# Splitting the float32 operands of the q, k and v projections into two float16 parts each, in a two-layer attention and router kernel

## The chip, the cores and the metric

The kernel runs on one core of a Trainium2 chip. The metric is the device time of one execution in microseconds (us); less is better. A core has a matrix engine (PE; its weight loads are shown apart as PEld), a vector engine (DVE), a scalar engine (ACT), a general-purpose engine (POOL) and an engine that issues DMA transfers (SP). Each engine works through its own instructions in order and waits where a semaphore is not yet up. A matrix product leaves its result in PSUM banks. POOL cannot read PSUM.

## The reference, cut to what matters

```python
x = x + A(layernorm(x));  x = x + B(layernorm(x))      # and the same pair once more
def A(x):            # 2048 tokens of 512, 32 heads of 16, one shared key and value head
    q = (x @ wq) per head;  k = x @ wk;  v = x @ wv
    p = softmax(q k^T * 16 ** -0.5);  return (p v) @ wo
def B(x):            # a router picks the 2 tokens with the greatest x . w_r
    return x + (a gated feed-forward net on these two tokens alone)
```

All inputs are float32.

## The kernel before, in words

The 2048 tokens are 16 tiles of 128. `xT` holds the normalised input transposed (four blocks of 128 features by 2048 tokens), `wq_sb` and `wkv_sb` the weights; all three are float32. Queries are needed in 16 groups `G` (4 chunks of 512 tokens by 4 groups of heads).

**Head.** Tiles are loaded, `in_stats` takes mean and variance on DVE and the reciprocal root (`rstd_of`, six small instructions) on POOL, `in_norm` normalises on DVE (`ln_x`), transposes on PE and copies to `xT` on ACT (`ln_t`). The tiles go in five groups: g0 and g1 of two tiles, g2 to g4 of four. After g1 the first query projection runs (`q_proj`, 256 tokens). After each chunk of four tiles `kv_piece` makes keys and values: PE, two ACT copies, one POOL subtraction (`kp`), then the keys go through DRAM (`k_store`, `k_spread`) into `k_st`. The piece of the last chunk is made in `early`, the first thing in layer 0.

**Stream of a layer.** 512 steps; in each, four score units (PE product, ACT exponential) and four units of row maxima (PE product `max_mm`, L458; DVE `reduce_max`, L469). A lead of eight steps has maxima alone. After every three score units (a run) PE does the products with the values (`pv_mm`, L557) and then, through `between`, at most one step of a pending piece: a step of the next query group (`q_piece`, four steps a piece, 60 pieces a layer) or of the output projection (`o_piece`). `by_columns` (L192) lays one step over the four column groups of PE. The order of all engines is that of the program text; nothing is rescheduled.

**Keys of chunk 1 less chunk 0.** `kd_x` subtracts inputs on POOL, `kd_tile` projects the difference; four tiles a layer.

**In layer 0 also** the tiles of layer 1 are normalised beside the stream (`next_x`, `ln_t`, `kv_piece`), the last four at its end. POOL does most of this. After the stream the router picks its two tokens (a gather from `xl_d`), the net runs, the two rows are normalised again, and layer 1 begins.

Float32 products are written as one instruction in the program and appear in the trace as two weight loads and two matmuls.

Of the kernel before, what the change touches and what calls it, by code (L numbers as in the profile page):

```python
# [17 lines left out]
P = 128  # L18
# [8 lines left out]
NG = 4  # L27
# [30 lines left out]
def interleaved_layers(ctx, tc, x_in, wq, wkv, wo, w_r, w_gate, w_up, w_down, out):  # L58
# [49 lines left out]
    xT = const.tile([P, NDC, S], F32, name="xT")  # L108
    wq_sb = const.tile([P, NDC, D], F32, name="wq_sb")
    wkv_sb = const.tile([P, NDC, P], F32, name="wkv_sb")  # L110
# [32 lines left out]
    def load_wq(w):  # L143
        return wq_sb[:, :, w], wq.rearrange("(c p) n -> p c n", p=P)[:, :, w]
# [30 lines left out]
    nc.gpsimd.memset(v_exts[0], 1.0)  # L175

# [91 lines left out]
    def kv_piece(c, pool=True):  # L268


        def step(k):
            def f(out, start, stop, shared):
                for j in range(TPC):
                    i = c * TPC + j
                    nc.tensor.matmul(out[32 * j:32 * (j + 1)], wkv_sb[:, k, 2 * DH:HR], xT[:, k, i * P:(i + 1) * P],
                                     start=start, stop=stop, skip_group_check=shared)
# [39 lines left out]
    def q_proj(G, w=slice(0, CW)):  # L316
# [18 lines left out]
    def q_piece(G, w):  # L335
# [3 lines left out]
        def step(k):  # L339
            def f(out, *flags):  # L340
                by_columns(out, wq_sb[:, k, g * P:(g + 1) * P], xT[:, k, c * CW + w.start:c * CW + w.stop], *flags)
# [13 lines left out]
    def k_direct(li, i):  # L355
# [3 lines left out]
        for k in range(NDC):  # L359
            nc.tensor.matmul(pk, wkv_sb[:, k, :], xT[:, k, w], start=k == 0, stop=k == NDC - 1)  # L360
# [10 lines left out]
    kds = {}  # L371

    def kd_x(li, j):

        w = slice(j * P, (j + 1) * P)
        kds[li, j] = xd = work.tile([P, NDC, P], F32, name="xh", bufs=3)
        nc.gpsimd.tensor_tensor(xd, xT[:, :, CW + w.start:CW + w.stop], xT[:, :, w], op=OP.subtract)

    def kd_tile(li, j):

        xd = kds.pop((li, j))
        w = slice(S + j * P, S + (j + 1) * P)
        pk = aux([P, P], F32)
        for k in range(NDC):
            nc.tensor.matmul(pk, wkv_sb[:, k, :], xd[:, k, :], start=k == 0, stop=k == NDC - 1)
        kf = work.tile([P, P], F32, name="kvf", bufs=2)
        nc.scalar.copy(kf, pk)
# [5 lines left out]
    def v_direct(li, i):  # L393
        w = slice(i * P, (i + 1) * P)
        pv = aux([P, DH], F32)
        for k in range(NDC):
            nc.tensor.matmul(pv, xT[:, k, w], wkv_sb[:, k, KQ:HR], start=k == 0, stop=k == NDC - 1)
# [15 lines left out]
    def layer(li, src_d, dst_d, early=None):  # L413
# [586 lines left out]
        for j in range(TPC):  # L1000
            at(T_KD + 2 * j, kd_x, li, j)
# [71 lines left out]
        if nxt:  # L1073
            ln_t(i - 2)
# [160 lines left out]
        ln_t(i - 1)  # L1235
        ln_t(i)
# [5 lines left out]
        for k in range(NDC):  # L1242
# [7 lines left out]
        xn = work.tile([P, NDC, 2], F32, name="xn", bufs=1)  # L1250
        nc.vector.tensor_copy(xn, pxn)
# [4 lines left out]
        for tok in toks:  # L1256
            of = nc.snap(tok // P)
            xb.append((of, work.tile([P, NDC, P], F32, name="xh", bufs=3)))
            nc.gpsimd.tensor_copy(xb[-1][1], xT[:, :, bass.ds(of * P, P)])
# [5 lines left out]
        for k in range(NDC):  # L1265
            nc.tensor.matmul(pk, wkv_sb[:, k, :], xn[:, k, :], start=k == 0, stop=k == NDC - 1)
# [14 lines left out]
        def v_again(of, x):  # L1281
            pv = aux([P, 1, DH], F32)
            for k in range(NDC):
                nc.tensor.matmul(pv[:, 0, :], x[:, k, :], wkv_sb[:, k, KQ:HR], start=k == 0, stop=k == NDC - 1)
# [16 lines left out]
    def in_norm(of):  # L1301
        for i in of:
            ln_x(i, xin[i], mvs[of], i - of[0], rss[of], nc.vector)
            ln_t(i)
# [17 lines left out]
    in_norm(g2)  # L1322
# [7 lines left out]
    in_norm(g3)  # L1330
# [3 lines left out]
    in_norm(g4)  # L1334
# [7 lines left out]

    number_tokens()
# [31 lines left out]
```

## Time and profile before

| | |
|---|---|
| median of 3 runs | 2670.74 us (2668.63 to 2672.21) |
| profiled execution | 2668.52 us |
| its span, first to last instruction | 2666.7 us |
| busy PE, DVE, ACT, POOL | 2611.8, 2496.2, 2336.5, 789.6 us |
| mean granted clock of PE | 0.987 of full speed |

Busy shares are means over a head, two streams and two tails. Matmuls overlap and their ends are modelled, so a busy PE is not one at its limit. A row of the trace gives the start, the length, the engine and line, the tiles written and read, how many were merged, and in brackets the idle time before and what ended it.

### The profile page before, as it was taken

How to read it: one execution, taken by the hardware profiler on the slowest of the kernel's cores; microseconds unless marked ns; L12 is line 12 of the kernel's file. 1: busy time of each engine (PE TensorE's matmuls, PEld its weight loads, DVE VectorE, ACT ScalarE, POOL GpSimd, SP SyncE). 2: the span in 40 equal slices, each digit the busy share in tenths (PEclk: the TensorE clock that was granted, in tenths of full speed). 3: DMA queues.
4: the chain of work that ended last, by engine and by line, in shares of the span. 5: the costliest groups of instructions: out<-in, count | busy, mean ns of one | idle time of the engine just before them, and what ended most of it. 6: DMA issues, size and time to landing. Idle time of an engine off the chain costs nothing.

```text
span 2666.7 us, 94903 instructions
## 1 busy us (share of the span) xinstructions
PE 2611.8 (98%) x39844; PEld 1264.3 (47%) x39844; DVE 2496.2 (94%) x4499; ACT 2336.5 (88%) x4874; POOL 789.6 (30%) x2144
## 2 busy tenths in 40 slices
PE   7999999999999999999999999999999999999999
PEld 3544444444444444444555444444444444444445
DVE  8999999999999999999679999999999999999995
ACT  2899999999999999999728999999999999999995
POOL 2211101234162433535522111012331424233363
PEclk7999999999999999999979999999999999999999
DMA  3001110000100001111400000000001000000114
GB/s 100 6 23 34 33 58 11 13 12 31 31 28 17 19 19 30 33 31 34 142 15 6 15 15 13 30 11 15 10 31 31 31 12 27 21 20 31 31 50 132
DMA packets 71344, 83.15 MB, mean 31 GB/s; under 512 B 27932, under 2 KB 44252, under 8 KB 70916
## 3 DMA queue, kind: packets, MB, share of 16 engines
q1 hardware_dynamic: 68050, 75.80, 9.4%
q8 instruction: 313, 5.13, 0.8%
q10 hardware_dynamic: 2354, 1.07, 0.1%
q14 instruction: 115, 0.94, 0.1%
q0 software_dynamic: 512, 0.20, 0.0%
HBM read 42.80 MB, written 17.18 MB: 22 GB/s over the span
## 4 chain that ended last, share of the span: by engine, by line
PE 68%; ACT 17%; POOL 5%; issue 5%; DMA 3%; DVE 2%; SPq 1%; ACTq 0%; DVEq 0%; POOLq 0%
PE pO L557 29%; PE pS L528 20%; ACT pr L530 13%; PE pM L458 9%; PE pO L192 5%; DMA q_st<-mr 1%; ACT wd L462 1%; SPq L507 1%; POOL xh L711 1%; ACT so L563 1%; ACT qf L687 1%; PE pS L192 1%; DVE mx L469 1%; DMA x<-xl_d,of 1%; POOL xh L773 0%
## 5 line engine op out<-in xcount | busy, mean ns | idle before, releaser
L469 DVE TENSOR_REDUCE mx<-pM 128x1 f32<-128x512 f32 x3784 | 2315.1, 680 | 86.4 <-PE pM L458 76.3
L530 ACT ACTIVATE pr<-pS 128x512 f32<-128x512 f32 x4044 | 2134.9, 609 | 183.7 <-PE pM L458 141.2
L458 PE MATMUL pM<-k_st,q_st 48*128 48x512 f16 x4096 | 1234.7, 386 | 7.3 <-DVE mx L469 3.3
L528 PE MATMUL pS<-q_st,k_st 50*128 50x512 f16 (+1 forms) x4248 | 1186.9, 371 | 21.4 <-DMA q_st<-mr 5.1
L557 PE MATMUL pO<-pr,v_ext 128*32 128x128 f32 (+1 forms) x22528 | 1174.2, 327 | 5.7 <-ACT so L563 2.2
L557 PEld LDWEIGHTS pO<-pr,v_ext 128*32 128x32 f32 x22528 | 561.8, 109 | 611.1 <-issue 387.7
L528 PEld LDWEIGHTS <-k_st 50*128 50x128 f16 x4352 | 298.6, 95 | 495.7 <-issue 371.6
L458 PEld LDWEIGHTS <-q_st 48*128 48x128 f16 x4096 | 295.8, 94 | 166.8 <-issue 133.6
L493 POOL TENSOR_SCALAR ma<-ma 128x8 f32<-128x8 f32 (+1 forms) x136 | 32.4, 238 | 834.4 <-DVE ma L488 627.5
L192 PE MATMUL pO<-xT,wq_sb 128*32 128x128 f32 x3840 | 192.6, 273 | 0.0
L688 POOL TENSOR_TENSOR x<-x,qf 128x128 f32<-128x128 f32 x128 | 58.3, 457 | 426.5 <-ACT qf L687 426.2
L192 PE MATMUL pO<-wo_sb,so 128*32 128x128 f32 x3328 | 162.0, 273 | 0.0
L350 POOL CAST qh<-qf 128x128 f16<-128x128 f32 x120 | 35.0, 292 | 423.6 <-ACT qf L349 423.6
L192 PEld LDWEIGHTS pO<-xT,wq_sb 128*32 128x32 f32 x3840 | 119.2, 110 | 34.4
L192 PEld LDWEIGHTS pO<-wo_sb,so 128*32 128x32 f32 x3328 | 102.4, 110 | 28.5
L711 POOL TENSOR_TENSOR xh<-xh 128x128 f32<-128x128 f32 (+7 forms) x384 | 98.6, 257 | 30.1
L466 DVE CUSTOM_DVE_ANT_0 wd<-pM,wd 128x512 f32<-128x512 f32 x156 | 106.1, 680 | 0.0
L462 ACT ACTIVATE wd<-pM 128x512 f32<-128x512 f32 x156 | 94.7, 607 | 0.0
L773 POOL TENSOR_TENSOR xh<-xh 128x256 f32<-128x256 f32 (+8 forms) x216 | 66.8, 309 | 15.0
L563 ACT COPY so<-pO 128x256 f32<-128x256 f32 (+1 forms) x136 | 54.3, 400 | 1.6 <-PE pO L557 1.5
L351 POOL TENSOR_TENSOR ql<-qf,qh 128x128 f16<-128x128 f32 x120 | 51.6, 430 | 9.7
L757 POOL TENSOR_SCALAR xh<-x,mv,rs 128x512 f32<-128x512 f32 x24 | 50.1, 2088 | 0.0
(268 smaller groups left out, 1061.9 us busy)
## 6 DMA issues: line engine op xcount, KB each, us to landing
q_st<-mr SPq DMA_DIRECT2D x512, 1.0 KB
zt<-zr_d SPq DMA_DIRECT2D x120, 64.0 KB
q_st<-qh SPq DMA_DIRECT2D x236, 32.0 KB
xl_d<-xh SPq DMA_DIRECT2D x28, 256.0 KB
pr<-in_w_up SPq DMA_DIRECT2D x12, 448.0 KB
x<-in_x SPq DMA_DIRECT2D x20, 256.0 KB
x_d<-x SPq DMA_DIRECT2D x16, 256.0 KB
x<-x_d SPq DMA_DIRECT2D x16, 256.0 KB
```

The lines of the kernel that those rows point to most:

```text
L192: nc.tensor.matmul(out[r], lhsT[:, r], rhs, start=start, stop=stop, skip_group_check=shared)
L458: nc.tensor.matmul(pm, q_st[u][r, j, q:q + P], k_st[r, kc * CW:(kc + 1) * CW], start=True, stop=True)
L462: nc.scalar.activation(rect, pm, AF.Relu)
L466: nc.vector.tensor_tensor_reduce(out=b_over_a, in0=pm, in1=b_over_a, scale=1.0, scalar=LOWEST, op0=OP.add, op1=OP.max, accum_out=mx[u][:, ...
L469: nc.vector.reduce_max(mx[u][:, c, i:i + 1], pm, axis=AX.X)
L528: nc.tensor.matmul(ps[:, k * 2 * w:(k + 1) * 2 * w], k_st[rows, kt * P:(kt + 1) * P], q_st[u][rows, :, b * w:(b + 1) * w], start=True, sto ...
L530: nc.scalar.activation(pr[hs][:, h, :], ps, AF.Exp, scale=DH ** -0.5)
L557: nc.tensor.matmul(po[u][32 * j:32 * (j + 1), b * w + q.start:b * w + q.stop], v_ext[:, kt, 1 - u % 2:33 - u % 2], p[:, j % 2, k, j // 2, ...
L563: nc.scalar.copy(so[u][:, b * w:(b + 1) * w], po[u][:, b * w:(b + 1) * w])
L688: nc.gpsimd.tensor_tensor(x1[i][:, w], x1[i][:, w], y, op=OP.add)
L711: g.tensor_tensor(t[:, :n], t[:, :n], t[:, n:2 * n], op=OP.add)
L773: nc.gpsimd.tensor_tensor(rp_t[i][:, :n], rp_t[i][:, :n], rp_t[i][:, n:2 * n], op=OP.add)
```

## The change

Every normalised input and weight of these projections is kept as a high and a low float16 part (low is the rest, rounded). A product becomes three float16 products: high by high, and the two mixed ones.

- Weights are loaded to staging tiles and split on POOL (`split_w`: a cast and a subtraction), `wkv` behind the first memsets, group 0 of `wq` before g2's `rstd_of`, groups 1 to 3 behind the head. The loads of groups 1 to 3 are three transfers in place of one.
- `ln_t` takes three forms. With `low=nc.vector` (g0, g1; the last two tiles of layer 0) ACT casts the high part and DVE subtracts from PSUM. With `low=nc.gpsimd` (g2 to g4; tile 13) ACT casts and copies, POOL subtracts. With none (in the stream) ACT copies once, POOL casts and subtracts.
- Query, key and value products run 12 float16 products where 4 float32 ones stood; `kd_x` is gone, `kd_tile` projects both chunks and POOL subtracts the two results.

```diff
-    xT = const.tile([P, NDC, S], F32, name="xT")
+    xT = const.tile([P, 2, NDC, S], HF, name="xT")
...
+    def split_w(name, dst):
+
+        w = staged.pop(name)
+        nc.gpsimd.tensor_copy(dst[:, 0], w)
+        nc.gpsimd.tensor_tensor(dst[:, 1], w, dst[:, 0], op=OP.subtract)
...
+    def by_parts(out, lhsT, rhs, start, stop, shared=False):
+
+        pairs = ((0, 0), (0, 1), (1, 0))
+        for n, (a, b) in enumerate(pairs):
+            by_columns(out, lhsT[:, a], rhs[:, b], start and n == 0, stop and n == len(pairs) - 1, shared)
+
+    def dot(out, lhsT, rhs, low_last):
+
+        pairs = ((0, 0), (1, 0), (0, 1)) if low_last else ((0, 0), (0, 1), (1, 0))
+        for n, (a, b) in enumerate(pairs):
+            for k in range(NDC):
+                nc.tensor.matmul(out, lhsT[:, a, k], rhs[:, b, k], start=n == k == 0, stop=n == 2 and k == NDC - 1)
...
-    def ln_t(i):
+    def ln_t(i, low=None):
+
         pT = aux([P, NDC, P], F32)
+        xh = xhs.pop(i)
         for c in range(NDC):
-            nc.tensor.transpose(pT[:, c, :], xhs[i][:, c * P:(c + 1) * P], ident)
-        nc.scalar.copy(xT[:, :, i * P:(i + 1) * P], pT)
-        del xhs[i]
+            nc.tensor.transpose(pT[:, c, :], xh[:, c * P:(c + 1) * P], ident)
+        hi, lo = (xT[:, a, :, i * P:(i + 1) * P] for a in range(2))
+        xh = xh.rearrange("p (c n) -> p c n", c=NDC)
+        if low:
+            nc.scalar.copy(hi, pT)
+        if low is nc.vector:
+            xh = pT
+        else:
+            nc.scalar.copy(xh, pT)
+        if not low:
+            nc.gpsimd.tensor_copy(hi, xh)
+        (low or nc.gpsimd).tensor_tensor(lo, xh, hi, op=OP.subtract)
...
-        for k in range(NDC):
-            by_columns(pq, wq_sb[:, k, g * P:(g + 1) * P], xT[:, k, c * CW + w.start:c * CW + w.stop],
-                       k == 0, k == NDC - 1)
+            by_parts(pq, wq_sb[:, :, k, g * P:(g + 1) * P], xT[:, :, k, c * CW + w.start:c * CW + w.stop],
+                     k == 0, k == NDC - 1)
...
-        nc.gpsimd.tensor_tensor(xd, xT[:, :, CW + w.start:CW + w.stop], xT[:, :, w], op=OP.subtract)
...
+        pk = aux([P, 2, P], F32)
+        dot(pk, wkv_sb, xT[:, :, :, :2 * CW].rearrange("p a c (t n) -> p a c t n", t=2)[:, :, :, :, j * P:(j + 1) * P],
+             True)
+        kf = work.tile([P, NDC, P], F32, name="xh", bufs=3)
+        nc.scalar.copy(kf[:, 0:2], pk)
+        nc.gpsimd.tensor_tensor(kf[:, 2], kf[:, 1], kf[:, 0], op=OP.subtract)
...
-        for k, tok in enumerate(toks):
-            nc.scalar.copy(xT[:, :, bass.ds(tok, 1)], pxn[:, :, k:k + 1])
+        xn = work.tile([P, 2, NDC, 2], HF, name="xn", bufs=1)
+        nc.vector.tensor_copy(xn[:, 0], pxn)
+        nc.vector.tensor_tensor(xn[:, 1], pxn, xn[:, 0], op=OP.subtract)
+        for k, tok in enumerate(toks):
+            nc.scalar.copy(xT[:, :, :, bass.ds(tok, 1)], xn[:, :, :, k:k + 1])
...
-    in_norm(g2)
+    in_norm(g2, nc.gpsimd)
...
+    for g in range(1, NG):
+        split_wq(g)
     number_tokens()
     layer(0, x_in, x2_d, early)
```

The order of POOL in the head, before, from the third chunk's key subtraction to the last chunk's (`kp`; `code` and `token` are small tables of token numbers):

```order
L286 TENSOR_TENSOR kp<-kvf,kp 128x128
L102 MEMSET code 128x3
L103 MEMSET token 128x3
L106 IOTA code 14x1 x2
L106 IOTA code 128x1 x2
L106 IOTA token 128x1 x2
L286 TENSOR_TENSOR kp<-kvf,kp 128x128
```

And of the change, at the same place (`so_158` to `so_162` are staged weights):

```order
L327 TENSOR_TENSOR kp<-kvf,kp 128x128
L303 TENSOR_TENSOR xT<-xh,xT 128x4x128 x4
L153 CAST wq_sb<-so_158 128x4x128
L154 TENSOR_TENSOR wq_sb<-so_158,wq_sb 128x4x128
L153 CAST wq_sb<-so_160 128x4x128
L154 TENSOR_TENSOR wq_sb<-so_160,wq_sb 128x4x128
L153 CAST wq_sb<-so_162 128x4x128
L154 TENSOR_TENSOR wq_sb<-so_162,wq_sb 128x4x128
L102 MEMSET code 128x3
L103 MEMSET token 128x3
L106 IOTA code 14x1 x2
L327 TENSOR_TENSOR kp<-kvf,kp 128x128
```

(Two rows of the number tables, which are as before, fall between the last two.) Ten POOL instructions of 512 elements a partition now stand between the two key subtractions.

The order of DVE in the head, before, where the first four tiles are normalised:

```order
L257 TENSOR_SCALAR xh<-pr,mv,rs 128x512 x2
L246 BN_STATS st<-pr 128x6
L247 BN_AGGR mv<-st 128x2
L246 BN_STATS st<-pr 128x6
L247 BN_AGGR mv<-st 128x2
L257 TENSOR_SCALAR xh<-pr,mv,rs 128x512 x2
```

And of the change (`xT<-pS,xT` is the subtraction from PSUM):

```order
L285 TENSOR_SCALAR xh<-pr,mv,rs 128x512
L303 TENSOR_TENSOR xT<-pS,xT 128x4x128
L285 TENSOR_SCALAR xh<-pr,mv,rs 128x512
L303 TENSOR_TENSOR xT<-pS,xT 128x4x128
L274 BN_STATS st<-pr 128x6
L275 BN_AGGR mv<-st 128x2
L274 BN_STATS st<-pr 128x6
L275 BN_AGGR mv<-st 128x2
L285 TENSOR_SCALAR xh<-pr,mv,rs 128x512
L303 TENSOR_TENSOR xT<-pM,xT 128x4x128
L285 TENSOR_SCALAR xh<-pr,mv,rs 128x512
L303 TENSOR_TENSOR xT<-pM,xT 128x4x128
```

A normalisation of the next tile now stands behind the subtraction of the tile before it.

## Rows read from the trace of the kernel before

**Rows 1.** The page's busy times and shares of the span, over the whole execution.

```profile
PE 2611.8 (98%) x39844; PEld 1264.3 (47%) x39844; DVE 2496.2 (94%) x4499; ACT 2336.5 (88%) x4874; POOL 789.6 (30%) x2144
```

**Rows 2.** Busy time of each engine in stretches of 50 us (the head, the start of the stream, two stretches within it, the tail of layer 0); behind the engines the granted clock, the DMA share and GB/s.

```profile
0.00:50.00 50.00, 32.53 (x290) 17.51 (x291) 37.41 (x80) 13.15 (x32) 18.96 (x70) 0.89 0.40 131
50.00:100.00 50.00, 49.35 (x748) 27.16 (x747) 49.03 (x86) 34.04 (x71) 5.87 (x19) 0.83 0.02 4
...
200.00:250.00 50.00, 49.52 (x750) 22.88 (x754) 49.37 (x89) 46.79 (x98) 4.26 (x17) 1.00 0.11 31
...
450.00:500.00 50.00, 49.72 (x784) 23.67 (x783) 48.36 (x87) 46.45 (x98) 6.04 (x21) 1.00 0.07 19
...
1350.00:1400.00 50.00, 47.22 (x371) 25.48 (x370) 39.09 (x78) 10.84 (x28) 7.65 (x22) 0.62 0.04 9
```

**Rows 3.** Who waited for whom, whole execution: us in total, times, longest.

```profile
DVE mx L469 <- PE pM L458: 76.3, 166, 1.1
...
PE pM L458 <- DVE mx L469: 3.3, 11, 0.6
```

**Rows 4.** POOL in the head, in order of time: the second memset, the key subtractions of chunk 0 and of the last chunk, and the first and the last of the six instructions of g3's reciprocal root.

```profile
5.36 0.53 POOL L175 MEMSET v_ext<- 128x528 f32 x1
...
19.08 0.64 POOL L286 TENSOR_TENSOR kp<-kvf,kp 128x128 f16<-128x128 f32 x1 [2.77 <-ACT kp L285]
19.80 0.29 POOL L221 TENSOR_SCALAR ve<-mv 128x4 f32<-128x4 f32 x1
...
22.27 0.20 POOL L226 TENSOR_TENSOR rs<-y,t 128x4 f32<-128x4 f32 x1
...
33.32 0.43 POOL L286 TENSOR_TENSOR kp<-kvf,kp 128x128 f16<-128x128 f32 x1 [3.36 <-DMA k_st<-k_d]
```

**Rows 5.** The other engines in the head, in order of time: normalisation, transposes and copy of the first tiles, the first query projection, the third chunk's keys, the start of the maxima.

```profile
10.82 0.97 DVE L257 TENSOR_SCALAR xh<-pr,mv,rs 128x512 f32<-128x512 f32 x2
11.39 1.97 PE L262 MATMUL pS<-ident,xh 128*128 128x128 f32 x8 [8.19 <-DVE xh L257]
...
12.54 0.59 ACT L263 COPY xT<-pS 128x512 f32<-128x512 f32 x1 [9.45 <-PE pS L262]
...
15.69 1.93 PE L192 MATMUL pM<-xT,wq_sb 128*32 128x256 f32 x32
...
26.22 1.88 PE L275 MATMUL pM<-xT,wkv_sb 128*32 128x128 f32 x32
...
33.81 9.65 DVE L469 TENSOR_REDUCE mx<-pM 128x1 f32<-128x512 f32 x16 [0.45 <-PE pM L458]
```

**Rows 6.** From the arrival of the last keys to the first exponential, in order of time (PEld rows are weight loads of four matmuls, one round of the query projection).

```profile
39.63 2.08 PE L458 MATMUL pM<-k_st,q_st 48*128 48x512 f16 x4 [0.31 <-DMA k_st<-k_d]
...
41.64 3.64 PE L192 MATMUL pS<-xT,wq_sb 128*32 128x256 f32 x32
42.07 0.20 PEld L192 LDWEIGHTS pS<-xT,wq_sb 128*32 128x32 f32 x4 [0.23 <-issue]
...
56.84 3.07 ACT L530 ACTIVATE pr<-pS 128x512 f32<-128x512 f32 x5 [6.69 <-PE pS L528]
```

**Rows 7.** Groups of instructions with shapes kept apart, whole execution: count, then busy us and mean ns of one, then idle before.

```profile
L192 PE MATMUL pO<-xT,wq_sb 128*32 128x128 f32 x3840 | 192.6, 273 | 0.0
L192 PEld LDWEIGHTS pO<-xT,wq_sb 128*32 128x32 f32 x3840 | 119.2, 110 | 34.4
...
L351 POOL TENSOR_TENSOR ql<-qf,qh 128x128 f16<-128x128 f32 x120 | 51.6, 430 | 9.7
L350 POOL CAST qh<-qf 128x128 f16<-128x128 f32 x120 | 35.0, 292 | 423.6 <-ACT qf L349 423.6
...
L377 POOL TENSOR_TENSOR xh<-xT 128x512 f32<-128x512 f32 x8 | 10.2, 1280 | 0.5
...
L674 DVE TENSOR_TENSOR x<-pS,x 128x512 f32<-128x512 f32 x6 | 4.1, 691 | 11.9 <-PE pS L192 11.9
```

**Rows 8.** One run of the stream on PE, in order of time: values, a query step, the next scores.

```profile
203.31 0.86 PE L557 MATMUL pO<-pr,v_ext 128*32 128x128 f32 x16
203.98 0.40 PE L192 MATMUL pO<-xT,wq_sb 128*32 128x128 f32 x8
204.32 0.39 PE L528 MATMUL pS<-q_st,k_st 50*128 50x512 f16 x1
```

**Rows 9.** One of DVE's gaps in the stream.

```profile
456.97 0.69 DVE L469 TENSOR_REDUCE mx<-pM 128x1 f32<-128x512 f32 x1 [0.61 <-PE pM L458]
```

**Rows 10.** POOL near the end of layer 0's stream, in order of time: it works without a pause from the first of these rows to the second.

```profile
1248.63 2.09 POOL L757 TENSOR_SCALAR xh<-x,mv,rs 128x512 f32<-128x512 f32 x1
...
1278.55 0.23 POOL L493 TENSOR_SCALAR ma<-ma 128x4 f32<-128x4 f32 x1 [1.08 <-DVE ma L488]
```

**Rows 11.** POOL between the layers: its last addition before the gather, and the gather.

```profile
1316.93 1.27 POOL L780 TENSOR_TENSOR x<-x,xh 128x512 f32<-128x512 f32 x1
1319.17 1.47 POOL L807 DMA_INDIRECT x<-xl_d,of  x1 [0.97 <-DVE of L805]
```

**Rows 12.** The chain that ended last, between the layers (start, us, what): the gather's transfer, a key product and a value product.

```profile
1319.17 8.89 DMA x<-xl_d,of
...
1330.45 1.71 PE pS L360 x8
...
1371.23 1.82 PE pS L397 x8
```

More of the change, by code (lines that the diff above doesn't have):

```diff
@@ L272, in f @@
             def f(out, start, stop, shared):
[L273 to L276, printed above, removed]
+                for n, (a, b) in enumerate(((0, 0), (1, 0), (0, 1))):
+                    for j in range(TPC):
+                        i = c * TPC + j
+                        nc.tensor.matmul(out[32 * j:32 * (j + 1)], wkv_sb[:, a, k, 2 * DH:HR],
+                                         xT[:, b, k, i * P:(i + 1) * P], start=start and n == 0, stop=stop and n == 2,
+                                         skip_group_check=shared)
             return f
@@ L340, in f @@
             def f(out, *flags):
-                by_columns(out, wq_sb[:, k, g * P:(g + 1) * P], xT[:, k, c * CW + w.start:c * CW + w.stop], *flags)
+                by_parts(out, wq_sb[:, :, k, g * P:(g + 1) * P], xT[:, :, k, c * CW + w.start:c * CW + w.stop], *flags)
             return f
@@ L358, in k_direct @@
         pk = aux([P, P], F32)
-        for k in range(NDC):
-            nc.tensor.matmul(pk, wkv_sb[:, k, :], xT[:, k, w], start=k == 0, stop=k == NDC - 1)
+        dot(pk, wkv_sb, xT[:, :, :, w], True)
         def parts():
@@ L369, in k_direct @@
         return parts
[L371 to L376, printed above, removed]
-        nc.gpsimd.tensor_tensor(xd, xT[:, :, CW + w.start:CW + w.stop], xT[:, :, w], op=OP.subtract)
     def kd_tile(li, j):
-        xd = kds.pop((li, j))
         w = slice(S + j * P, S + (j + 1) * P)
[L383 to L387, printed above, removed]
+        pk = aux([P, 2, P], F32)
[4 more added lines that the diff above has]
+        nc.gpsimd.tensor_tensor(kf[:, 2], kf[:, 1], kf[:, 0], op=OP.subtract)
+        kf = kf[:, 2]
         for h in range(2):
@@ L395, in v_direct @@
         pv = aux([P, DH], F32)
-        for k in range(NDC):
-            nc.tensor.matmul(pv, xT[:, k, w], wkv_sb[:, k, KQ:HR], start=k == 0, stop=k == NDC - 1)
+        dot(pv, xT[:, :, :, w], wkv_sb[:, :, :, KQ:HR], False)
         nc.scalar.copy(v_exts[li][:, i, 1:32:2], pv)
@@ L1257, in layer @@
             of = nc.snap(tok // P)
-            xb.append((of, work.tile([P, NDC, P], F32, name="xh", bufs=3)))
-            nc.gpsimd.tensor_copy(xb[-1][1], xT[:, :, bass.ds(of * P, P)])
+            xb.append((of, work.tile([P, 2, NDC, P], HF, name="xh", bufs=3)))
+            nc.gpsimd.tensor_copy(xb[-1][1], xT[:, :, :, bass.ds(of * P, P)])
         q_st.clear()
@@ L1264, in layer @@
         pk = aux([P, 2], F32)
-        for k in range(NDC):
-            nc.tensor.matmul(pk, wkv_sb[:, k, :], xn[:, k, :], start=k == 0, stop=k == NDC - 1)
+        dot(pk, wkv_sb, xn, True)
         for h in range(2):
@@ L1282, in v_again @@
             pv = aux([P, 1, DH], F32)
-            for k in range(NDC):
-                nc.tensor.matmul(pv[:, 0, :], x[:, k, :], wkv_sb[:, k, KQ:HR], start=k == 0, stop=k == NDC - 1)
+            dot(pv[:, 0, :], x, wkv_sb[:, :, :, KQ:HR], False)
             nc.vector.tensor_copy(v_exts[li + 1][:, bass.ds(of, 1), 1:32:2], pv)
@@ L1299, in in_stats, with in_norm @@
                 rss[of] = rstd_of(mvs[of], len(of))
-    def in_norm(of):
+    def in_norm(of, low):
         for i in of:
             ln_x(i, xin[i], mvs[of], i - of[0], rss[of], nc.vector)
-            ln_t(i)
+            ln_t(i, low)
     g0, g1, g2, g3, g4 = groups
@@ L1308, in interleaved_layers @@
     in_stats(g1, g1)
+    split_wq(0)
     in_stats(g2[:2], g2)
-    in_norm(g0)
+    in_norm(g0, nc.vector)
     in_stats(g2[2:], g2)
-    in_norm(g1)
+    in_norm(g1, nc.vector)
     w = slice(0, 2 * P)
@@ L1341, in early @@
         k_spread(0, 3)
+    for g in range(1, NG):
+        split_wq(g)
     number_tokens()
```

32 lines of the change are left out of this document (17 added, 15 removed).

## The prediction

> **What bounds the kernel now.** I read the busy times first: PE 98%, DVE 94%, ACT 88% [rows 1]. A PE row's end is modelled, so I looked next at stretches of the stream. There DVE works 49.37 us of 50 where only query steps run beside it and 48.36 where output steps run too [rows 2]. The waits agree: DVE waited 76.3 us in all for the products of the maxima, PE 3.3 us for DVE to free a bank [rows 3]. So DVE sets the pace of the stream; PE is next, and costs DVE 0.6 to 1.6 us in 50. One such gap is 0.61 us [rows 9]. In the head it is otherwise: DVE is busy 37.41 us of the first 50, POOL 18.96, PE's clock averages 0.89 and then 0.83 of 2.4 GHz [rows 2]. There a chain counts: inputs, normalised tiles, keys, maxima, scores. What is added to that chain is added to the time, since a stream that runs at 97% of DVE catches up with nothing.
>
> **Head, first four tiles.** Before, DVE issues two normalisations in 0.97 us and goes on; the query projection starts at 15.69, 4.87 us after the first of them (10.82) [rows 5]. Now DVE subtracts from PSUM behind each tile, and the next tile's normalisation stands behind that subtraction. A tile then takes: 0.57 from normalisation to transposes (10.82 to 11.39), 1.15 to ACT (12.54), 0.59 ACT [rows 5], and the subtraction, which I price as the one DVE row that reads PSUM and SBUF, 0.69 [rows 7]: 3.0 us. Four tiles and two pairs of statistics between (0.8 each) are 13.6 in place of 4.87: **+8.7**. POOL's two early weight splits end in time: a 512-element subtraction is 1.28 [rows 7]; a cast of 128 elements is 0.29 against 0.43 for a subtraction [rows 7], and by that ratio one of 512 is about 0.65 (an estimate). A split is then 2.0 us; the first starts at 5.89 [rows 4] if its 256 KB have come (no row shows when), and both lie beside the slow DVE chain. So the projection starts at about 24.4.
>
> **Head, POOL from the first to the last key subtraction.** Before, these end at 19.72 and 33.75 [rows 4]. The first now ends some 9 us later, at 28.7. What follows is serial on POOL: reciprocal root of g3 2.7 (19.80 to 22.47 [rows 4]); four subtractions 4 × 1.28 = 5.1; the key piece, which needs the last of them (PE about 1.9 [rows 5], ACT and POOL 0.8), 2.7; root of g4 2.7; 5.1; 2.7; then g4, whose transposes stand behind the key piece on PE, so that POOL waits about 1.7 for its first tile; 5.1; three weight splits, 3 × 1.9 = 5.8; number tables and the last key subtraction 1.5. That is 35.1, and the last keys are subtracted at 63.8 in place of 33.75: **+30.0**. Behind it everything runs as before: store, spread, PE's wait for the keys (ends 39.63), first exponential at 56.84 [rows 6]. Two things come off. DVE still had about 2.3 of the 16 maxima before the last keys to do at 39.63 (33.81 onwards, 0.6 each [rows 5]); now they are done: −1.4. And the second query projection, at half clock, goes from 16 passes of 256 columns (a round of two passes is 0.43 [rows 6]) to 12: −0.85. DVE can't start its maxima until the fifteenth normalisation, which waits for a buffer, near 55; 16 of 0.6 still end before the keys come. Sum for the head: **+27.7**. Bounds: PE at full clock and cheap casts (0.5, 1.1) shorten the serial part to +22; half clock all through gives +31.
>
> **Stream, query steps.** 120 pieces of four steps are 480 steps. A step is 8 matmul records now [rows 8]; it covers 0.40 us and one record lasts 273 ns [rows 7], so its two rounds of four start 0.11 apart (0.40 − 0.273, less 0.02 of stagger within a round). A round is two passes over 128 columns, 107 ns at 2.4 GHz. Float16 needs three one-pass rounds, 0.16, where two take 0.22, and the last record ends 0.05 earlier: 0.1 saved a step if the next weights load behind a pass of 53 ns. That no row shows: the loads here last 110 ns and hide behind a round as long [rows 7]. If a round can't be shorter than a load, three take 0.33 and a step costs 0.1 more. I take the saving, since the 110 seems to hold a latency that overlaps: the four loads of a round cover only 0.20 together even at half clock [rows 6]. Little of it reaches the end: DVE's gaps at PE's hands are 76.3 us in 166 waits [rows 3], a third of runs hold a query step, and a gap of 0.61 shrinks by 0.1 at most: **−4**, bounds −10 and +25 (480 × 0.11, half of it caught by PE's slack).
>
> The Trainium skill speaks against the saving ("TensorE: Matmul & The Clock Gate", section Back-to-back issue gap): a stream of load and matmul pairs settles at about 81 ns a matmul of 128 columns, set by both. And "TensorEngine Tiling (Array Packing)", Restrictions and Gotchas, rules out fast weight loads with column tiling. By that a step would be 0.24 against 0.22, and the −4 become about +5; no row here shows it.
>
> **Stream of layer 0, normalisation on POOL.** Each tile adds a cast and a subtraction, 1.9 us. For chunks 0 and 1 POOL stands idle behind them. For chunk 2 it works without a pause from 1248 to 1277 [rows 10]; three tiles add 5.7 us against 1.08 of idle time, and the last key piece and the last maxima of the stream come later: **+1**, 0 to +3. The key-difference tiles exchange a POOL subtraction of 512 for one of 128 elements, eight times: 0.
>
> **Between the layers.** Tile 12's cast and subtraction stand ahead of the gather on POOL: it ended its addition at 1318.2, so the gather goes from 1319.17 to 1320.2 [rows 11], and its 8.89 us lie on the chain [rows 12]: +1.0. Two subtractions on DVE ahead of the two rows' normalisation: +1.4; the split of those rows +0.4. Key products (1.71 for eight records, weight loads of 128 float32 columns) get shorter where they are on the chain: −0.8; value products at half clock, 1.82 each [rows 12], have 16 columns and cost loads alone; six of them, partly under DVE's maxima: −2. Net **0**, −3 to +4.
>
> **Sum.** 27.7 − 4 + 1 + 0 = +24.7 on the profiled execution's 2668.5 is 2693. That execution lies 2.2 below the median of the runs, so I say **2695**. About 0.2% (5.3 us) is what a measurement of this kernel can tell from no change.
>
> **The rivals.**
> *PE's share is worth more (faster).* The place is the stream: if all 480 steps gave 0.1 to the end, −48 + 28.7 gives 2651. It decides in favour of the change once the stream returns more than 28.7 us, 0.06 a step. For it: PE at 98% and DVE's 76.3 us of waits, the most there is to win. Against: DVE at 97 to 99%, and gaps that mostly fall where no query step stands. Chance 0.09.
> *The head's additions are hidden (within 0.2%).* Were the lead's maxima the bound, late keys would cost nothing: 2671 to 2675. For it: DVE is busy without a break from 33.81. Against: those maxima need the keys, and DVE's own normalisations now wait for POOL. 0.07.
> *Query steps get no shorter.* Three rounds take the 0.22 of the two now, or a little more, because loads and passes hinder each other: head and tails +28.7, stream 0 to +10, 2699 to 2709. For it: loads hide today behind passes twice as long. 0.20. The page named above would have it so.
> *Rounds wait for loads of 110 ns.* +0.1 a step, half of it felt: 2668.5 + 28.7 + 25 + 2.2 = 2724. 0.08.
> *My forecast,* 2683 to 2709 by its own bounds (not all of them at once): 0.56.
>
> From 2681 to 2715 about 0.8 is held: the forecast, nearly all of the third rival, and the low edge of the fourth not. Faster 0.09, same 0.07, slower 0.84.
>
> **What would show it.** In the changed profile the first query projection should start near 24, POOL's last key subtraction end near 64, the first exponential stand near 84, with POOL busy some 40 us of the first 65. In the stream, three query rounds should start 55 ns apart, the next scores 0.25 us behind the step's start instead of 0.34, DVE's busy share in 50 us unchanged to a few tenths. The gather should be issued about 1 us later behind the last scores. I am wrong if the first exponential comes before 70, if POOL's 512-element subtractions to float16 take much under 1.28, or if DVE's share of the stream falls or rises by more than 0.5 us in 50.

## The result and the profile after

| | before | after |
|---|---|---|
| median of 6 runs | 2671.01 us (2668.63 to 2672.80) | 2691.66 us (2690.75 to 2694.13) |
| ratio | | 1.0079, 95% interval 1.0067 to 1.0092 |
| span of the profiled execution | 2666.7 us | 2689.6 us |

The changed kernel is slower by 20.6 us. Busy times, the waits on the maxima, and the stretches that answer to [rows 1 to 3] (the page's first part; who waited for whom; windows of 50 us):

```profile
PE 2604.1 (97%) x42032; PEld 1280.6 (48%) x42032; DVE 2503.9 (93%) x4506; ACT 2341.3 (87%) x4887; POOL 830.9 (31%) x2193
```

```profile
DVE mx L501 <- PE pM L490: 81.9, 161, 2.9
```

```profile
0.00:50.00 50.00, 20.29 (x251) 15.12 (x252) 25.40 (x54) 14.32 (x32) 29.20 (x70) 0.87 0.37 120
50.00:100.00 50.00, 39.37 (x340) 16.41 (x341) 39.48 (x67) 15.32 (x32) 12.83 (x28) 0.58 0.05 13
...
450.00:500.00 50.00, 49.52 (x825) 23.82 (x822) 48.49 (x87) 46.71 (x98) 5.12 (x21) 1.00 0.05 12
```

The totals say little. The first two stretches do: DVE falls from 37.41 and 49.03 to 25.40 and 39.48, POOL rises from 18.96 and 5.87 to 29.20 and 12.83. The head has grown, and it waits for POOL. In the stretch at 450 DVE's share moved by 0.13.

**Where the time went.** A layer has 2048 exponentials of 512 columns on ACT (L530 before, L562 after). Counted in order, from 0, their starts are marks that both traces share:

| mark | before, us | after, us | difference | since the mark above |
|---|---|---|---|---|
| layer 0, exponential 0 | 56.84 | 84.28 | +27.44 | +27.44 head |
| 128 | 144.81 | 173.52 | +28.71 | +1.27 |
| 1792 | 1157.10 | 1181.13 | +24.03 | -4.68 |
| 2047, the last | 1321.39 | 1348.44 | +27.05 | +3.02 end of layer 0 |
| layer 1, exponential 0 | 1386.17 | 1412.75 | +26.58 | -0.47 between |
| 128 | 1475.09 | 1501.75 | +26.66 | +0.08 |
| 1792 | 2479.35 | 2501.35 | +22.00 | -4.66 |
| 2047 | 2639.11 | 2661.65 | +22.54 | +0.54 |
| end of the last instruction that counts as busy | 2664.06 | 2687.12 | +23.06 | +0.52 |

The head of the changed kernel, in order of time (answers to [rows 4 to 6]):

```profile
10.85 0.52 DVE L285 TENSOR_SCALAR xh<-pr,mv,rs 128x512 f32<-128x512 f32 x1
13.19 0.69 DVE L303 TENSOR_TENSOR xT<-pS,xT 128x512 f16<-128x512 f32 x1 [1.82 <-ACT xT L296]
13.80 0.54 DVE L285 TENSOR_SCALAR xh<-pr,mv,rs 128x512 f32<-128x512 f32 x1
...
22.96 2.75 PE L207 MATMUL pM<-xT,wq_sb 128*32 128x256 f16 x48
...
27.56 0.43 POOL L327 TENSOR_TENSOR kp<-kvf,kp 128x128 f16<-128x128 f32 x1 [6.31 <-ACT kp L326]
...
30.78 3.56 POOL L303 TENSOR_TENSOR xT<-xh,xT 128x512 f16<-128x512 f32 x3
35.22 1.15 POOL L303 TENSOR_TENSOR xT<-xh,xT 128x512 f16<-128x512 f32 x1 [0.88 <-ACT xh L300]
...
56.45 0.61 POOL L153 CAST wq_sb<-so 128x512 f16<-128x512 f32 x1
...
60.73 1.15 POOL L154 TENSOR_TENSOR wq_sb<-so,wq_sb 128x512 f16<-128x512 f32 x1
...
62.72 0.44 POOL L327 TENSOR_TENSOR kp<-kvf,kp 128x128 f16<-128x128 f32 x1
...
68.68 1.10 PE L490 MATMUL pM<-k_st,q_st 48*128 48x512 f16 x4 [3.98 <-DMA k_st<-k_d]
69.72 2.75 PE L207 MATMUL pS<-xT,wq_sb 128*32 128x256 f16 x48
...
84.28 3.08 ACT L562 ACTIVATE pr<-pS 128x512 f32<-128x512 f32 x5 [6.65 <-PE pS L560]
```

The second normalisation stands 2.95 us behind the first, behind the subtraction; the chunks' key subtractions end at 27.99 and 63.16. Groups of instructions and one run of the stream (answers to [rows 7, 8]):

```profile
L207 PE MATMUL pO<-xT,wq_sb 128*32 128x128 f16 x5760 | 168.0, 219 | 0.0
L207 PEld LDWEIGHTS <-wq_sb 128*32 128x32 f16 x6000 | 143.5, 98 | 41.5 <-issue 2.8
...
L303 POOL TENSOR_TENSOR xT<-xh,xT 128x512 f16<-128x512 f32 x26 | 30.7, 1189 | 6.2 <-ACT xh L300 5.2
```

```profile
231.85 0.86 PE L589 MATMUL pO<-pr,v_ext 128*32 128x128 f32 x16
232.53 0.35 PE L207 MATMUL pO<-xT,wq_sb 128*32 128x128 f16 x12
232.81 0.39 PE L560 MATMUL pS<-q_st,k_st 50*128 50x512 f16 x1
```

From a step's start to the next scores it is 0.28 us where it was 0.34. The median from a step's start to PE's next product (the step's cover), over some 470 of the 480 steps, is 0.283 against 0.334, and rounds start 0.056 apart.

### The profile page after: what moved, and what is told of

It is laid out like the page before. It is cut to its first block, busy times and chain, and to the rows that moved or that the text cites. A ratio compares the mean times of both kernels' runs of the same rounds, so it can differ in the third digit from the quotient of the medians.

```text
span 2689.6 us, 99346 instructions
## 1 busy us (share of the span) xinstructions
PE 2604.1 (97%) x42032; PEld 1280.6 (48%) x42032; DVE 2503.9 (93%) x4506; ACT 2341.3 (87%) x4887; POOL 830.9 (31%) x2193
## 4 chain that ended last, share of the span: by engine, by line
PE 71%; ACT 17%; POOL 4%; issue 3%; DMA 2%; DVE 2%; SPq 1%; ACTq 0%; DVEq 0%; POOLq 0%
PE pO L589 31%; PE pS L560 22%; ACT pr L562 13%; PE pM L490 10%; PE pO L207 5%; ACT wd L494 1%; DMA q_st<-mr 1%; ACT so L595 1%; SPq L539 1%; DVE mx L501 1%; ACT qf L719 1%; PE pS L207 1%; DMA x<-xl_d,of 1%; PE pS L220 0%; POOL xh L743 0%
## 5 line engine op out<-in xcount | busy, mean ns | idle before, releaser
L562 ACT ACTIVATE pr<-pS 128x512 f32<-128x512 f32 x4044 | 2135.5, 610 | 178.4 <-PE pM L490 134.9
L490 PE MATMUL pM<-k_st,q_st 48*128 48x512 f16 x4096 | 1250.3, 387 | 12.1 <-DMA k_st<-k_d 4.0
L560 PE MATMUL pS<-q_st,k_st 50*128 50x512 f16 (+1 forms) x4248 | 1191.9, 371 | 24.4 <-DMA q_st<-mr 4.1
L207 PE MATMUL pO<-xT,wq_sb 128*32 128x128 f16 x5760 | 168.0, 219 | 0.0
L207 PEld LDWEIGHTS <-wq_sb 128*32 128x32 f16 x6000 | 143.5, 98 | 41.5 <-issue 2.8
L805 POOL TENSOR_TENSOR xh<-xh 128x256 f32<-128x256 f32 (+8 forms) x216 | 66.7, 309 | 15.0
```

Source lines behind the costliest of these rows:

```text
L490: nc.tensor.matmul(pm, q_st[u][r, j, q:q + P], k_st[r, kc * CW:(kc + 1) * CW], start=True, stop=True)
L560: nc.tensor.matmul(ps[:, k * 2 * w:(k + 1) * 2 * w], k_st[rows, kt * P:(kt + 1) * P], q_st[u][rows, :, b * w:(b + 1) * w], start=True, sto ...
L562: nc.scalar.activation(pr[hs][:, h, :], ps, AF.Exp, scale=DH ** -0.5)
L805: nc.gpsimd.tensor_tensor(rp_t[i][:, :n], rp_t[i][:, :n], rp_t[i][:, n:2 * n], op=OP.add)
```

## The experiments

The changed kernel and the six experiments that keep its head (two of them with a round more or less in the two projections) have their first exponential between 84.23 and 85.61, 85.1 in the mean. A head is read with that scatter in mind. From mark 128 to mark 1792 the kernels with the query steps of the changed one differ from the kernel before by −4.2 to −4.9 us; the first 64 exponentials of a layer and the end of layer 0 scatter by 1 us and more.

**The head.** `e1_splits_late`: the three weight splits behind the last key piece.

```diff
-    for g in range(1, NG):
-        split_wq(g)
     number_tokens()
...
         k_spread(0, 3)
+        for g in range(1, NG):
+            split_wq(g)
```

> The three weight splits of groups 1 to 3 go behind the last key piece on POOL; nothing else changes. My theory (the head is a serial chain on POOL, and the splits, 56.45 to 61.88 in the changed kernel, stand in it): the last key subtraction ends near 57.7 instead of 63.2, the first exponential falls from 84.3 to about 79.5 (DVE's sixteen maxima that need no late keys, from 54.5 to 64.2, take over as the last 1 us), the total is about 2687 instead of 2691.7. Rival (DVE or PE at half clock sets the head, POOL only follows): the last keys come earlier but the first exponential stays above 82, total within 2 us of the changed kernel.

Measured: 2689.12 us, ratio 1.0072 (1.0055 to 1.0089). On DVE and ACT:

```profile
59.93 9.66 DVE L501 TENSOR_REDUCE mx<-pM 128x1 f32<-128x512 f32 x16 [2.18 <-PE pM L490]
```

```profile
82.32 3.08 ACT L562 ACTIVATE pr<-pS 128x512 f32<-128x512 f32 x5 [6.64 <-PE pS L560]
```

The last keys are subtracted 3.65 us earlier (59.51), but the first exponential comes only 2.0 us earlier (2.8 before the mean above). PE no longer waits for the keys; DVE now works at the maxima without a break from 59.93 to 69.6. So a second chain, the maxima behind the late fifteenth normalisation, stood 2 to 3 us behind the chain of the keys. Both theories are half right: the first exponential stays above 82, as the rival said, but it lies below the scatter, and the total falls by 2.5 us, more than the rival allowed.

`e9_lag4`: in the first four tiles DVE subtracts one tile behind (`rest` is the subtraction).

```diff
             ln_x(i, xin[i], mvs[of], i - of[0], rss[of], nc.vector)
-            ln_t(i, low)
+            if rest:
+                rest()
+            rest = ln_t(i, low, low is nc.vector)
```

> Of the changed kernel only the order on DVE over the first four tiles: the subtraction of a tile from PSUM stands behind the normalisation of the next one instead of ahead of it. My theory (the first term of the sum, 8.7 us for a chain of 3.0 us a tile, shifts all that follows): first query projection near 18.7 instead of 23.0, every later mark earlier by about 4.3, first exponential near 80, total 2687.5. Rival (POOL's long serial part absorbs it, the start of the chain does not matter): projection earlier but first exponential above 83, total 2691.

Measured: 2687.12 us, ratio 1.0067 (1.0051 to 1.0082).

```profile
18.61 1.98 PE L207 MATMUL pM<-xT,wq_sb 128*32 128x256 f16 x48
...
57.92 0.44 POOL L331 TENSOR_TENSOR kp<-kvf,kp 128x128 f16<-128x128 f32 x1
```

```profile
79.48 3.08 ACT L566 ACTIVATE pr<-pS 128x512 f32<-128x512 f32 x5 [6.65 <-PE pS L564]
```

The projection starts 4.35 us earlier, the last key subtraction 4.80, the first exponential 4.8. The theory holds: what starts late in this chain ends late.

`e2_sub_on_pe`: no subtraction on DVE or POOL in the head. Behind the transposes:

```diff
+        nc.scalar.copy(hi, pT)
+        def rest():
+            nc.tensor.matmul(pT, minus, hi, start=False, stop=True, skip_group_check=True)
+            nc.scalar.copy(lo, pT)
```

> In the head the low part is made without DVE and POOL: ACT casts the high part from PSUM, PE adds minus the high part to the same bank (a product with a negative float16 identity), ACT casts the rest; the second half of a tile stands behind the transposes of the next one. The splits stay where they are. My theory (twelve subtractions of 1.19 on POOL and the chain of DVE subtractions over the first four tiles carry 14.3 + 8 of the 27.4 us): query projection starts near 17.5 instead of 23.0, last key subtraction ends near 45 instead of 63.2, first exponential near 66 (62 to 70), total 2668 to 2678. Rival (the head is held by PE at half clock and by the inputs, so that work taken from POOL comes back on ACT and PE): first exponential above 74, total above 2681.

Measured: 2669.85 us, ratio 0.9996 (0.9986 to 1.0006). The output of this kernel is wrong, so its low parts are not the rests (the last section has the likely reason); the work and its order are as told.

```profile
28.62 0.60 PE L312 MATMUL pM<-ident,xh 128*128 128x128 f32 x4
...
39.28 0.44 POOL L343 TENSOR_TENSOR kp<-kvf,kp 128x128 f16<-128x128 f32 x1
```

```profile
62.07 3.08 ACT L578 ACTIVATE pr<-pS 128x512 f32<-128x512 f32 x5 [6.64 <-PE pS L576]
```

22 of the head's 27.4 us are gone with those subtractions, although ACT and PE now do that work: more than the theory's 18, since the last key subtraction ends at 39.72 and not near 45. The path behind the keys, with PE at half clock, is no rival: from the last key subtraction to the first exponential it takes 23.1 us before, 21.1 after and 22.4 in this kernel, so the whole difference lies ahead of it. This is the strongest evidence for the first two terms of the sum.

`e5_head` should do the same with a sum that adds up, and more:

```diff
-            nc.tensor.transpose(pT[:, c, :], xh[:, c * P:(c + 1) * P], ident)
+            nc.tensor.matmul(pT[:, c, :], xh[:, c * P:(c + 1) * P], ident, start=c == 0, stop=False, skip_group_check=True)
...
+    in_norm_of(g3, 0, 1)
     whole(kv_piece, 1, False)
```

> The head of the second experiment, with three differences: the transposes are ordinary products with the identity that open one accumulation in the bank, so that the product with the negative identity adds to all of it; the splits of groups 1 to 3 stand behind the last key piece; the first tile of a chunk is transposed ahead of the key piece of the chunk before. In the second experiment the three key pieces after the first were 6.4 us apart, with ACT (eight casts of 0.5 us a chunk) idle from 24.9 to 27.1 for the key piece. My theory (the head's price is serial work in the chain of the keys; 5.2 us of it were left): first exponential near 59.5 (58 to 61), total 2665 to 2669. Rival (casts on ACT bound the head now, the order does not matter): first exponential at 62 or later, total 2670.

Measured: 2672.04 us, ratio 1.0002 (0.9992 to 1.0011), first exponential at 65.21: by the number the rival, but ACT's casts are not what grew. A tile's four transposes now cost 1.05 us on PE:

```profile
30.82 1.05 PE L312 MATMUL pM<-ident,xh 128*128 128x128 f32 x8
```

As ordinary float32 products they are eight records where the transposes were four in 0.60. The three gaps between the key pieces on ACT are 8.1, 7.3 and 5.9 us, where they were 6.4, 6.4 and 6.5. That PE's longer transposes are the cause is my reading; no run takes them out alone. Even so this kernel, whose sum does add up, is rid of 19.1 of the head's 27.4 us, in part by the late splits.

`e10_mix` gives POOL and DVE the subtraction by turns (DVE one tile behind), with the late splits and, below, the order and buffers of `e6_ring`.

```diff
-            ln_t(i, low)
+            if low is nc.vector or i % 2:
+                rest = ln_t(i, nc.vector, True)
+            else:
+                ln_t(i, low)
```

> A version that gives the right result with all three reliefs that the runs so far speak for: in the head ACT casts the high part, and the subtraction goes by turns to POOL and to DVE (there one tile behind), splits of groups 1 to 3 behind the last key piece, order and buffers of tiles 8 to 10 as in the sixth experiment. By the parts: head +4 to +6 against the kernel before, query steps -9.3, key differences +2.5, end of layer 0 +1.3: 2668 to 2672, no difference from the kernel before that can be measured. Rival (DVE or ACT becomes the head's bound, as PE's transposes did in e5): first exponential above 66, total above 2675.

Measured: 2677.89 us, ratio 1.0029 (1.0017 to 1.0040), first exponential at 72.55: the rival. DVE, in order, waits for ACT's cast of each tile that it subtracts, and reaches the maxima at 48.04:

```profile
39.57 0.69 DVE L304 TENSOR_TENSOR xT<-pM,xT 128x512 f16<-128x512 f32 x1 [1.89 <-ACT xT L296]
...
48.04 12.04 DVE L505 TENSOR_REDUCE mx<-pM 128x1 f32<-128x512 f32 x20
```

**Query steps.** `e4_four` adds a fourth round, `e11_two` drops the third.

```diff
-        pairs = ((0, 0), (0, 1), (1, 0))
+        pairs = ((0, 0), (0, 1), (1, 0), (1, 1))
```

> A query step gets a fourth round, low part by low part, which the output does not need (the two head projections too, under 0.5 us). A step's cover on PE should go from 0.283 to 0.339 us. What the end of the stream feels of it, over the 480 steps (27 us of PE): by the reasoning of my prediction (DVE sets the pace, a twelfth of PE's time reaches the end) +2 us; by the ratio that the change itself showed (12.2 us of PE saved a layer, 4.65 given back) 38%, +10 us; if PE were the bound, +27 us.

```diff
-        pairs = ((0, 0), (0, 1), (1, 0))
+        pairs = ((0, 0), (0, 1))
```

> A query step has two rounds instead of three (the product of the weights' low part with the inputs' high part is left out, in the head's two projections too). Cover on PE 0.227 instead of 0.283 us, 13.4 us a layer less. If 38% of PE's time reaches the end here as well, each layer's query steps give 5.1 us more (9.8 against the kernel before). If DVE alone sets the pace once PE has this much slack, they give under 2 us more.

Measured: 2706.09 us, ratio 1.0134 (1.0118 to 1.0151), and 2680.09 in one run. A step of each on PE:

```profile
200.85 0.41 PE L207 MATMUL pO<-xT,wq_sb 128*32 128x128 f16 x16
201.19 0.39 PE L560 MATMUL pS<-q_st,k_st 50*128 50x512 f16 x1
```

```profile
199.81 0.29 PE L207 MATMUL pO<-xT,wq_sb 128*32 128x128 f16 x8
200.03 0.39 PE L560 MATMUL pS<-q_st,k_st 50*128 50x512 f16 x1
```

| rounds of a step | cover, us (median) | exponentials 128 to 1792 against before, layers 0 and 1 |
|---|---|---|
| float32 (before) | 0.334 | 0 |
| four | 0.339 | +0.67, +0.44 |
| three (after) | 0.283 | -4.68, -4.66 |
| two | 0.227 | -8.82, -8.68 |

A layer has 240 steps, and 214 of them lie between these two marks. (The expectations reckoned with all 240, and so with 38%.) There the change took 214 × 0.051 = 10.9 us of PE and gave back 4.7: 43%. The fourth round's 12.0 us cost 5.2 (44%), the middle one of its three answers; the third round's 12.0 are worth 4.1 (34%), in a single run. So the share hardly changes upwards and falls as PE gets slack.

**Key differences.** `e7_kd` projects differences made on POOL, `e12_kd_high` leaves the mixed products out.

```diff
+        g.tensor_tensor(d, xT[:, 0, :, b], xT[:, 0, :, a], op=OP.subtract)
+        g.tensor_tensor(d, d, xT[:, 1, :, b], op=OP.add)
+        g.tensor_tensor(d, d, xT[:, 1, :, a], op=OP.subtract)
+        g.tensor_copy(xd[:, 0], d)
+        g.tensor_tensor(xd[:, 1], d, xd[:, 0], op=OP.subtract)
...
+        dot(pk, wkv_sb, kds.pop((li, j)), True)
```

> Differences of keys from differences of inputs again: POOL takes the high parts' difference, adds and subtracts the low parts, splits the result (five instructions of 512 elements a tile, about 5.5 us), and PE runs twelve products of 128 columns a tile in place of twelve of 256, 0.64 us in place of 1.28 (four float32 products took 0.43). My theory (of PE's time in the stream 38% reaches the end; the four tiles cost 1.0 to 1.3 us a layer): exponentials 0 to 128 of each layer lose 0.3 to 0.6 us in place of 1.0 to 1.3. Rival (the price is not PE's but that of ACT's and POOL's work behind these products, or POOL's 22 us of new work delay the row maxima): they lose 1 us or more.

```diff
+        for k in range(NDC):
+            nc.tensor.matmul(pk, wkv_sb[:, 0, k], x01[:, k], start=k == 0, stop=k == NDC - 1)
```

> In the key differences the two mixed products are left out (four products of 256 columns a tile, 0.43 us of PE, as much as the four float32 ones took; ACT and POOL work as in the changed kernel); the output lacks those parts. My theory (the 1.0 to 1.3 us that the four tiles cost a layer is PE's time, 0.85 us a tile more, of which 38% reaches the end): exponentials 64 to 128 of each layer lose 0 to 0.2 us against the kernel before in place of 1.03. Rival (the price is ACT's larger copy and POOL's subtraction behind the products): they lose 0.7 us or more.

Measured: 2693.45 and 2683.76 us, one run each. One tile's products before, after, in `e7_kd` and in `e12_kd_high`:

```profile
103.62 1.16 PE L385 MATMUL pS<-xh,wkv_sb 128*128 128x128 f32 x8
```

```profile
131.31 1.49 PE L220 MATMUL pS<-xT,wkv_sb 128*128 128x256 f16 x12
```

```profile
131.95 0.84 PE L220 MATMUL pS<-xh,wkv_sb 128*128 128x128 f16 x12
```

```profile
132.74 0.61 PE L417 MATMUL pS<-xT,wkv_sb 128*128 128x256 f16 x4
```

Both expectations had the float32 products at 0.43 us; the row says 1.16. Over exponentials 64 to 128, where the four tiles stand, the changed kernel loses 1.03 us in each layer, with 4 × 0.33 more on PE, and `e12_kd_high` gains 2.47 in each, with 4 × 0.55 less. ACT's copy and POOL's work are the same in both, so the price is PE's, and there nearly all of it reaches the end, not 38%. `e7_kd` has 4 × 0.32 less on PE and still loses 0.82 in layer 0 and 2.08 in layer 1. It gains 0.3 to 0.5 at each of exponentials 66, 72 and 81, as PE's shorter products would have it, and loses all at the 90th (2.2 and 2.5) and, in layer 1, the 93rd (1.2). There POOL's five instructions stand ahead of the maxima's last steps, and ACT waits for what PE makes of them, so the theory and the second half of the rival both hold:

```profile
1480.22 0.25 ACT L546 CAST mr<-pM 16x128 f16<-16x128 f32 x1 [2.44 <-PE pM L544]
```

```profile
1477.99 1.15 POOL L423 TENSOR_TENSOR xh<-xh 128x512 f16<-128x512 f32 x1
1479.11 0.24 POOL L536 TENSOR_SCALAR ma<-ma 128x8 f32<-128x8 f32 x1
```

**End of layer 0.** Of the 3.0 us, 2.8 are lost at the 1980th exponential. There ACT stood in the changed kernel:

```profile
1301.57 0.81 ACT L870 ACTIVATE xh<-x,rs_c,rs 128x512 f32<-128x512 f32 x1 [2.65 <-POOL x L812]
```

ACT normalises the next tile in its turn among the exponentials, and waits for an addition that stood on POOL behind the cast and subtraction of the tile before. `e3_end_order`:

```diff
-                    at(t + 2, ln_t, i)
+                    at(t + 2 + (c == NCH - 2), ln_t, i)
```

> For the third chunk of layer 0 the transposes, the cast and the subtraction of a tile of layer 1 come one step later, so that on POOL they stand behind the addition of the next tile instead of ahead of it. My theory (of the 3.0 us that the end of layer 0's stream lost, nearly all is ACT's normalisation of the next tile, which waits 2.65 us for that addition behind 1.8 us of cast and subtraction): the last 128 exponentials of layer 0 take 2 to 3.5 us less than in the changed kernel, total about 2689. Rival (POOL is simply full there, 5.4 us of new work against 1.1 us of idle time, and the order does not matter): less than 1 us comes back.

`e6_ring` has this line too, and:

```diff
-                xhs[i] = work.tile([P, D], F32, name="xh", bufs=3)
+                name, n = ("wd", 4) if i % TPC < TPC - 1 else ("xh", 3)
+                xhs[i] = work.tile([P, D], F32, name=name, bufs=n)
```

> As the third experiment (cast and subtraction of a tile behind the next tile's addition), and the normalised tiles 8 to 10 get buffers of their own (those of the late weights) in place of a ring of three that the router's tiles share. There ACT waited 2.82 us for POOL's subtraction, which still read the buffer that the next normalisation writes. My theory (order and buffer together were the wait): ACT's normalisation no longer waits over 0.5 us, and exponentials 1920 to 2047 of layer 0 lose under 1 us against the kernel before, where the changed kernel lost 3.0. Rival (POOL is full): they lose 2 us or more.

Measured: 2695.17 us, ratio 1.0089 (1.0072 to 1.0106), and 2691.62 in one run. Their ACT at this place:

```profile
1303.60 0.81 ACT L870 ACTIVATE xh<-x,rs_c,rs 128x512 f32<-128x512 f32 x1 [2.82 <-POOL xT L303]
```

```profile
1301.50 0.81 ACT L871 ACTIVATE wd<-x,rs_c,rs 128x512 f32<-128x512 f32 x1 [1.30 <-POOL x L812]
```

With the order alone the wait is as long and its releaser another: the subtraction still read the buffer that the normalisation writes. The theory of `e3_end_order` failed: the end of layer 0 lost 4.3 us, not less than 3.0. With buffers apart the wait halves. At the 1980th exponential the loss is 2.8 us in the changed kernel and in all eight experiments that leave this place alone, 3.0 with the order alone, and 1.5 in all three that have order and buffers. So order and buffer together are half of this wait; the other half is again a wait for POOL's addition, and that POOL is simply full there was not tested.

The whole end of layer 0 is less clear. From 1792 to 2047 the nine kernels that leave this place alone lose 2.7 to 4.1 us. `e6_ring` loses 1.4, but `e10_mix` and `e8_best`, which have its lines too, lose 2.3 and 4.6, in part at other exponentials. What sets those was not looked into.

**All together.** `e8_best` has the head of `e5_head`, `e6_ring`, `e7_kd`, and `ln_t` of tile 12 two steps later:

```diff
-            at(e + 8, ln_t, i)
+            at(e + 10, ln_t, i)
```

> All of these together (head of e5, order and buffers of e6, key differences of e7), and the cast and subtraction of tile 12 behind the gather. By the sum of the parts: head +2.5, query steps -9.3, key differences +1, end of layer 0 +0.5, between the layers -1 against the kernel before, -6: total 2665 (2662 to 2668), faster than both. Rival (what one part gives back another takes: DVE sets the pace and the head's lead only moves): 2669 or more.

Measured: 2675.45 us, ratio 1.0012 (1.0003 to 1.0021). By the number this is the rival: it beats the changed kernel, not the one before. But the rival's reason does not show. The query steps gave back what was summed; what failed were the prices of the other parts: the head costs 9.6 us and not 2.5 (first exponential at 66.48), the key differences 2.1 and 3.3 us over exponentials 64 to 128 of the two layers and not 1 together, and the end of layer 0 4.6 and not 0.5. No version that leaves nothing out beats the kernel before; `e5_head` can't be told from it.

## Why the prediction held, point by point

**Which resource sets the head: right.** The first key subtraction was to end at 28.7 and ended at 27.99; from there to the last one 35.1 us were summed and 35.2 measured; the first exponential was to stand near 84. Inside this sum terms were off against each other: a subtraction takes 1.19, not 1.28 (−1.1 over twelve), and POOL waits 0.9 us for the fourth tile of each chunk, which the sum lacks. The projection began at 22.96, not 24.4: it starts before the fourth tile's subtraction has ended. After the last keys arrive 15.6 us remain where it had been 17.2; −2.25 was forecast and −1.6 came. `e2_sub_on_pe` and `e9_lag4` show that the chain carries the time. POOL was busy 40.2 us of the first 65, as forecast. But the sum can't be read backwards: `e1_splits_late` took 5.4 us of splits out and got 2.0 to 2.8, because the maxima follow close behind.

**Query steps: direction right, −4 against −9.3.** Two terms were mis-sized, and partly made up for each other. The step lost 0.051 us, not 0.1: the rounds are 56 ns apart as forecast, but the last round's tail to the next scores (0.171) is longer than one round. And 43% of it reaches the end, where the waits of DVE for PE had made me take a twelfth. The failed step is "Little of it reaches the end": the waits of one engine are not the price. Two reasons can be read, and no run separates them. ACT too waited for PE, and for longer than DVE, in the trace of before:

```profile
ACT pr L530 <- PE pM L458: 141.2, 462, 2.2
```

And a step sits just in the runs that PE makes long. Over exponentials 256 to 1023 of layer 0, from the start of one run's products with values to the next, 109 runs with a query step last 1.889 us before and 1.864 after, 98 runs with no step 1.677 and 1.683. Some of the 109 hold more values or scores as well; among runs that are otherwise alike (74 and 92) it is 1.821 against 1.662 before. So the step of 0.334 us made a run 0.16 longer, 48% of itself: that was in the trace of before, and is the number to read. It would have given 480 × 0.051 × 0.48 = 11.8 us, near the 9.3.

**The rivals fell.** The stream returned 9.3 us and not 28.7, and the head's 27.4 us were not hidden. Three rounds take 0.168 us with loads of 98 ns each, so loads and passes of four column groups do overlap. The Trainium skill's "TensorE: Matmul & The Clock Gate", section Back-to-back issue gap, gives 81 ns a matmul for a stream of load and matmul pairs of 128 columns. The prediction took that figure for a round of four column groups, of which the section says nothing; the trace disagrees with it there, with four matmuls started every 56 ns.

**Key differences: 0 against +2.1.** I weighed POOL's exchange of instructions and left PE's out: twelve products of 256 columns for four float32 ones of 128, 1.49 against 1.16 us a tile.

**End of layer 0: +1 against +3.0,** at the edge of the bounds. POOL's 5.7 us were nearly right, three times 1.8 measured; wrong was who waits. I looked at the key piece and the maxima behind POOL, and not at ACT, whose normalisation in the middle of the exponentials needs POOL's addition and a buffer that the new subtraction holds longer.

**Between the layers: 0 against −0.5, open.** The gather is issued 1.16 us ahead of the last exponential's start where it had been 2.22 ([rows 11]), the forecast +1.0:

```profile
1347.28 1.47 POOL L839 DMA_INDIRECT x<-xl_d,of  x1 [0.22 <-issue]
```

The whole stretch can't be settled: in the changed kernel and the nine experiments that keep it, it takes 62.1 to 66.7 us from the last exponential to the next first one, 64.8 before. In layer 1 the first 64 exponentials give back 0.95 us and the key differences then take 1.03; the 0.95 were not looked into, and other kernels with the same stream give back 0.2 to 0.5 there.

**The sum:** +23.1 between the marks, +24.7 forecast; 2691.7 against 2695. The head was foreseen in its parts. That the rest came so near is in part luck: the query steps gave 5.3 us more than forecast, and the key differences and the end of layer 0 took 4.1 more.

## What to carry to other kernels

A new instruction on an engine that idles on average is free only where no chain runs through that engine: in the head, what stood on POOL between the key subtractions went into the time, until the next chain took over (`e1_splits_late`). In the stream's middle the same casts and subtractions cost nothing that can be seen: layer 0, which has them, gained 4.68 us from mark 128 to 1792, and layer 1, which has none, 4.66. To price work on the second engine of a stream, compare the length of otherwise equal runs with and without that work, not the bound engine's waits. And when a reader of a ring buffer changes, look for who writes that buffer next, on every engine.

## What the runs showed of the hardware that was not expected

- A round of four float16 products of 32 weight columns and 128 moving columns starts every 56 ns although each weight load lasts 98; at four rounds a step the spacing holds (0.339 us).
- In `e2_sub_on_pe` a product without the start flag stands behind four float32 transposes into one bank, and the output is wrong; in `e5_head`, with the bank opened once by an ordinary product, it is right. The Trainium skill's "PSUM — Partial Sum Buffer", rule 2 of The four PSUM rules, offers a reason: a matmul that starts a group clears the written marks of the whole bank, and a later product without the start flag overwrites where a mark is clear. The pair of runs agrees with that if each transpose starts a group; no run here shows the marks, and the pair changes the kind of instruction along with the flags.
- Four float32 transposes take 0.60 us in four records; the same as products with the identity take 1.05 in eight.
- PE's granted clock was 0.50 (1.2 GHz) from 60 to 84 us in the changed kernel, whose PE had been busy 5.78 of the 10 us before. In `e2_sub_on_pe` it was 1.00 (2.4 GHz) up to 40 us, with PE busy 7.2 to 7.5 of each 10 from 10 us on, and then fell to 0.64 and 0.50 although PE was busier (8.76 of the 10 us from 40 to 50). And the column does not tell all: in the changed kernel the 48 products of a query projection take 2.75 us at 22.96 and again at 69.72, with 1.00 in the column of the one stretch and 0.50 in that of the other; in `e2_sub_on_pe` they take 1.49 at 16.99, with 1.00. Why is open.
